# Order of weight loads, and queues of one pair's C and x, in a fused Mamba-2 scan and bilinear feed-forward kernel

## Chip, cores and metric

The kernel runs on one core of one Trainium2 chip. The metric is the device time of one execution in microseconds (us). Three runs of the kernel before gave 122.89, 122.69 and 123.45 us, median 122.89.

## What is computed

The inputs are `x` (4 batches, 8 heads, 768 tokens, 32 channels), a decay `a` per token, `B` and `C` (16 states per token and head), and three weights of a feed-forward layer. The first half is a state-space scan. The reference runs it in chunks of 32 tokens:

```python
for c in range(nc):                                   # chunks of the sequence
    cum = np.cumsum(la, axis=-1)                      # la = log a of the chunk
    L = np.exp(cum[..., :, None] - cum[..., None, :]) * causal
    M = np.einsum('bhin,bhjn->bhij', Cc, Bc) * L
    y[:, :, sl] = M @ xc + einsum('bhin,bhnd->bhid', Cc, state) * exp(cum)[..., None]
    state = decay_full * state + sum_j Bc[j] (x) xc[j] * decay_from_j[j]
```

The second half takes all heads of a token as one row of 256 numbers and gives `(row @ w_a) * (row @ w_b) @ w_out`, with 1536 hidden columns. The output is 3072 rows of 256.

## The kernel before, in words

The kernel cuts the sequence into 6 blocks of 128 tokens (instead of chunks of 32) and the 4 batches into two pairs of batches. A "pair" p = 2 * block + (batch pair) is the unit of the scan, so there are pairs 0 to 11. Pairs 0 to 3 (blocks 0 and 1) go one by one; later ones go block by block. The change touches pairs 2 and 3 and what stands around them.

For a pair of blocks 0 and 1 the stages are these.

- Loads: B, C and x each come in two transfers, one for each batch (`load1`, L157, transfers recorded at L165).
- `scale_bc` (L370, recorded at L379) multiplies B by the inverse decay (result `bm`) and C by the decay (result `cm`). For pairs 2 and 3 GpSimd does this.
- `transposes` (L386, recorded at L409) turns `bm` and `cm` on TensorE, two matmuls with the identity each, into a PSUM bank. ScalarE copies B out twice (`bt`, L413), VectorE copies C out (`ct`, L429). An argument `between` is called between the turn of B and the turn of C; whatever it issues on TensorE stands between them.
- `scores` (L437, recorded at L458) makes 32 small matmuls of turned B and C into four banks, SC[0] to SC[3]. `mask` (L490) multiplies them by the causal mask: three quarters by VectorE (L497), the last quarter by a ScalarE copy and GpSimd (L494, L495).
- `scale_x` (L357) rounds x to 16 bits. For pair 3 it is GpSimd's work (L368), for pair 2 ScalarE's (L366).
- `pv` (L555) multiplies with the carried state (L562), with x (L518), and makes the pair's own state (`ds_mm`, L545). `state_sums` (L646) and `state_spread` (L658, GpSimd, recorded at L662 and L677) carry the state on.

For the feed-forward half, `unit(p, k2)` (L726) makes two of the 12 hidden slices of a pair: four matmuls with Wa (`aps`), four with Wb (`bps`, all at L691), a ScalarE copy of the first (`asb`, L715) and a product by VectorE (`hk`, L722). `out_mm` (L734, recorded at L737) multiplies `hk` by Wo. Wo is loaded in two halves (`load_wo`, L219, recorded at L220): half 0 holds hidden slices 0 to 5, half 1 slices 6 to 11. Three of the output products of pairs 0 and 1 are made in two passes: first 18 matmuls with half 0, then, after `pv(2)`, 18 with half 1.

The order of the work is written by hand (`manual_schedule`): each engine executes its own instructions in the order of the source, and semaphores hold an instruction until its operands are there. GpSimd and SyncE also issue transfers in that order, and a transfer that waits holds what is queued behind it. For the stretch of interest that order, before the change, is:

- GpSimd: B and C of pair 2 (four transfers), three small state factors `hr`, `hs`, `hsx` (L909 to L911), Wo half 0, x of pair 2 (two transfers), the scalings of pair 2, Wo half 1, the spread of pair 0's state, x of pair 3 (two transfers, in `scores2`), the masked quarter of pair 2, four transfers that spread decay rows (`spread_rows`, L339), the scalings of pair 3, the spread of pair 1's state, and the rounding of pair 3's x.
- SyncE: the decay rows to memory (L334), then B of pair 3, which waits by an explicit dependence until Wo half 0 has landed, C of pair 3, and the C and B of later blocks (`rq` at L183, `bn` at L174).
- TensorE: the state factors' matmul into `gps` (L931), the state matmuls of pairs 0 and 1 (L545), units of pair 0, turn of B and of C of pair 2, unit (1, 3) and so on.

Of the kernel before, what the change touches and what calls it, by code (L numbers as in the profile page):

```python
# [29 lines left out]
def kernel(  # L30
# [13 lines left out]
    nc = tc.nc  # L44
# [34 lines left out]
    indm = c32[:, 0:128]  # L79
# [8 lines left out]
    Wa = [big.tile([128, 2, KC], f16, name=f"Wa{t}") for t in range(2)]  # L88
    Wb = [big.tile([128, 2, KC], f16, name=f"Wb{t}") for t in range(2)]
# [24 lines left out]
    hsx = big.tile([128, nb, NG], f32, name="hsx")  # L114
# [23 lines left out]
    def bank(name):  # L138
        return psf.tile([128, 512], f32, name=name, tag=f"ff{next(banks)}")
# [17 lines left out]
    def load1(eng, p, which, bt, i0=0, n=64):  # L157
        blk, bp = divmod(p, NBP)
        if p >= P0:
            return eng.dma_start(  # L160
                by_token(pair_in[p][which])[:, bt],
                (B, C, x)[which][2 * bp + bt, :, blk * Q : (blk + 1) * Q, :].rearrange("h q n -> q h n"),
            )
        src = (B, C, x)[which][2 * bp + bt, :, blk * Q + 2 * i0 : blk * Q + 2 * i0 + 2 * n, :]
        return eng.dma_start(  # L165
            pair_in[p][which][64 * bt + i0 : 64 * bt + i0 + n].rearrange("i h r n -> i h (r n)"),
            src.rearrange("h (i r) n -> i h (r n)", r=2),
        )
# [50 lines left out]
    def load_wo(half):  # L219
        return nc.gpsimd.dma_start(  # L220
            Wo[:, 6 * half : 6 * half + 6].rearrange("p (g kk) e -> p g (kk e)", kk=3),
            moe_w_out.rearrange("(g p kk) e -> p g (kk e)", p=128, kk=3)[:, 2 * half : 2 * half + 2],
        )
# [146 lines left out]
    def scale_bc(p, which, eng, factor=None):  # L370
        blk, bp = divmod(p, NBP)
        name = ("bm", "cm")[which]
        if p >= P0:
            f = (fBl, fCl)[which][:, blk - P0 // NBP].rearrange("p (b t h) -> p b t h", b=NBP, t=2)[:, bp]
        else:
            f = (f_c(blk) if which else fB[:, blk])[:, :, bp]
        raw = by_token(pair_in[p][which]) if p >= P0 else pair_in[p][which].rearrange("p h r n -> p r h n")
        m_ = pre.tile([128, 2, H, N], f16, name=name, tag=name, bufs=4 if which else None)
        eng.tensor_tensor(  # L379
            out=m_,  # L380
            in0=raw,
            in1=(f if factor is None else factor).unsqueeze(3).broadcast_to((128, 2, H, N)),
            op=ALU.mult,
        )
        st.setdefault(p, {})[name] = m_
    def transposes(p, ps=None, between=None, apart=False):  # L386
        s = st.setdefault(p, {})
        blk, bp = divmod(p, NBP)
        if p >= P0:
            if by_block(blk, 0):  # L390
                TB = st[("turned", p, 0)].rearrange("p t q -> p (t q)")
            else:
                tr = bank("tr").bitcast(f16)
                TB, TC = tr[:, 0:256], tr[:, 256:512]
        elif ps is None:
            ps = [bank("tb") if p == 1 else SC[0], SC[2] if p == 3 else SC[1]] if apart else None
            on_dve = apart
            TB, TC = (TT[:, 0:256], TT[:, 256:512]) if ps is None else [t_.bitcast(f16)[:, 0:256] for t_ in ps]
        else:
            on_dve = True  # L400
            TB, TC = [t_.bitcast(f16)[:, 0:256] for t_ in ps]
        BT = mid.tile([128, 2, 2, 2, 64], f16, name="bt", tag="bt")
        if not by_block(blk, 1):
            CT = mid.tile([128, 2, Q], f16, name="ct", tag="ct")
        b_ = []

        def turn(T_, src):
            for r in range(2):
                nc.tensor.transpose(T_[:, r * 128 : (r + 1) * 128], src[:, r].rearrange("p h n -> p (h n)"), ident)  # L409

        def copy_bt(e):
            o_ = BT[:, e].rearrange("p r t i -> p (r t i)")
            b_.append(nc.scalar.activation(out=o_, in_=TB, func=AF.Copy, scale=par[:, e : e + 1]))  # L413

        if not by_block(blk, 0):
            turn(TB, s["bm"])
        if between:
            between()
        if not by_block(blk, 1):
            turn(TC, s["cm"])  # L420
        copy_bt(0)
        copy_bt(1)
        if p >= P0:
            if not by_block(blk, 1):
                nc.scalar.copy(CT.rearrange("p t q -> p (t q)"), TC)
                s["CT"] = CT
            s["BT"] = BT.rearrange("p e r t i -> p e r (t i)")
            return
        c_ = (nc.vector.tensor_copy if on_dve else nc.scalar.copy)(  # L429
            CT.rearrange("p t (i r) -> p r (t i)", r=2), TC.rearrange("p (r c) -> p r c", r=2)  # L430
        )
        if apart:
            for i_ in b_:
                tc.declare_no_dep(c_.ins, i_.ins.name, reason="reads of two banks")
        s["BT"], s["CT"] = BT, CT
# [92 lines left out]
    def ds_mm(p, c0, banks):  # L528
        s = st[p]
        s["DS"] = [b_[:, c0 : c0 + 2 * D] for b_ in banks]  # L530
        for bt, m in itertools.product(range(2), range(4)) if p >= P0 else ():
            nc.tensor.matmul(
                s["DS"][bt][32 * m : 32 * m + 32, :],
                s["bm"][:, bt, 2 * m : 2 * m + 2, :].rearrange("p h n -> p (h n)"),
                by_token(s["X16"])[:, bt, 2 * m : 2 * m + 2].rearrange("p h d -> p (h d)"),
                start=True,
                stop=True,
                skip_group_check=True,
                tile_position=(0, 32 * m),
            )  # L540
        for r in range(2) if p < P0 else ():
            for m in range(4):
                for bt in range(2):
                    k = slice(64 * bt, 64 * bt + 64)
                    nc.tensor.matmul(  # L545
                        s["DS"][bt][32 * m : 32 * m + 32, :],
                        s["bm"][k, r, 2 * m : 2 * m + 2, :].rearrange("p h n -> p (h n)"),
                        s["X16"][k, 2 * m : 2 * m + 2, r, :],
                        start=(r == 0),
                        stop=(r == 1),  # L550
                        skip_group_check=True,
                        tile_position=(64 * bt, 32 * m),
                    )
# [159 lines left out]
    def evac_a(a_ps, on_dve=False):  # L713
        asb = ffh.tile([128, 512], f32, name="asb", tag="asb", bufs=5)
        (nc.vector.tensor_copy if on_dve else nc.scalar.copy)(asb, a_ps)  # L715
        return asb

    def times(p, k2, b_ps, asb):
        s = st[p]
        if "hk" not in s:  # L720
            s["hk"] = ffh.tile([128, NK, 2 * Q], f16, name="hk", tag="hk")
        nc.vector.tensor_tensor(  # L722
            out=s["hk"][:, 2 * k2 : 2 * k2 + 2, :].rearrange("p k q -> p (k q)"), in0=b_ps, in1=asb, op=ALU.mult
        )
# [97 lines left out]
    def loads_x(p, eng=None):  # L822
        if p < NP:
            load2(eng or nc.gpsimd, p, 2)
# [7 lines left out]
    def go(*items):  # L832
        for p, k2 in items:
            unit(p, k2)()
# [55 lines left out]
    asb = [evac_a(aps[0])]  # L890
# [15 lines left out]
    nc.scalar.copy(maskbd, headm.unsqueeze(2).broadcast_to((128, H, D)))  # L906
    over_mid(2, NBLK)
    times(0, 0, bps[0], asb[0])
    nc.gpsimd.tensor_tensor(out=hr, in0=Pr[:, 0:NG, Q - 1], in1=rmid[:, 0:NG], op=ALU.mult)  # L909
    nc.gpsimd.tensor_tensor(out=hs, in0=hr, in1=Pr[:, 1:NBLK, 63], op=ALU.mult)  # L910
    nc.gpsimd.tensor_tensor(  # L911
# [2 lines left out]
        in1=selb.rearrange("p (b g) -> p b g", b=nb),  # L914
        op=ALU.mult,
    )
    wo0 = load_wo(0)
    for bt in range(2):
        load1(nc.gpsimd, 2, 2, bt)
    times(0, 1, bps[1], asb[1])  # L920
    times(0, 2, bps[2], asb[2])
    scale_bc(2, 0, nc.gpsimd)
    scale_bc(2, 1, nc.gpsimd)
    load_wo(1)
    go((1, 0))
    unit(1, 1, ps=(SC[0], None))()
    late_rows(nc.vector)
    rows = store_rows(nc.sync)
    go((1, 2))
    gps = SC[0][:, 256 : 256 + nb * NG]  # L930
    nc.tensor.matmul(gps, indm, hsx.rearrange("p b g -> p (b g)"), start=True, stop=True, skip_group_check=True)  # L931
    for p in range(NBP):
        ds_mm(p, 2 * D * p, SC[:2])
    nc.scalar.copy(G.rearrange("p b g -> p (b g)"), gps)
    state_sums(0)
    state_sums(1)
    state_spread(0)
    b3 = [load1(nc.sync, 3, 0, bt) for bt in range(2)]
    tc.add_manual_dep(b3[0].ins, wo0.ins.name, AFTER, reason="weights ahead of pair 3's inputs")
    for bt in range(2):  # L940
        load1(nc.sync, 3, 1, bt)
    loads_bc(4)
    loads_bc(5)
    aps = [unit_mm(0, 3, Wa), unit_mm(0, 4, Wa)]
# [1 line left out]
    for k2 in (3, 4):  # L946
        times(0, k2, unit_mm(0, k2, Wb), asb[k2 - 3])
    go((0, 5))
    transposes(2, apart=True)
    go((1, 3))  # L950
    def scores2():
        scores(2)
        loads_x(3)
        mask(product(2, 3), by_pool=True)
        spread_rows(nc.gpsimd, rows)

# [236 lines left out]
```

## Time and profile before

| | us |
|---|---|
| median of three runs | 122.89 |
| the profiled execution, its own time | 123.49 |
| the span of its instructions | 121.8 |
| TensorE matmul busy (PE) | 116.1 |
| VectorE busy (DVE) | 93.9 |
| ScalarE busy (ACT) | 76.0 |
| GpSimd busy (POOL) | 70.3 |

The profile shows one execution. PE is TensorE's matmul row and PEld its weight loads; DVE, ACT, POOL and SP are VectorE, ScalarE, GpSimd and SyncE; a q behind an engine's name is its queue of transfers. A row of the timeline has start, duration, engine, source line, operation, the result's name and, after `<-`, the operands, how many instructions are merged in the row, and in brackets how long the engine was idle before it and what ended that. Starts count from the first instruction. A matmul's end is modelled and reaches into the next one's start, so distances between starts are the safer measure. A row of the window sums has the window's length, the busy time of each engine, the granted TensorE clock (1.00 is full) and the share of time that the core's 16 DMA engines were busy. A row of the issues has a transfer's result and source, the issuing queue, the count, the size of one, and the time from issue to landing. The granted clock is 1.00 in every window used here.

### The profile page before, as it was taken

To read this page: it belongs to the slowest core of one execution; us is meant where nothing else is said; L and a number is where in the kernel's file an instruction comes from. 1 tells how busy PE (TensorE), PEld (TensorE's weight loads), DVE (VectorE), ACT (ScalarE), POOL (GpSimd) and SP (SyncE) were. 2 spreads that over 40 slices of the span, in tenths; PEclk is the share of its full clock that TensorE was granted. 3 is DMA by queue.
4 is the path that set the end of the run, shared out by engine and by line. 5 is a ranking of instruction groups with operands and counts; after the bars stand their busy time and mean duration, and the time that the engine had idled before them with its cause. 6 is when DMAs were issued, how large, how long until landed. Compare 5 with 4: busy or idle time off the path is not lost.

```text
span 121.8 us, 3715 instructions
## 1 busy us (share of the span) xinstructions
PE 116.1 (95%) x1436; PEld 78.9 (65%) x1436; DVE 93.9 (77%) x185; ACT 76.0 (62%) x155; POOL 70.3 (58%) x96
## 2 busy tenths in 40 slices
PE   6899799999999999999999999999999999999990
PEld 2255699887898898744476464766464784555890
DVE  4999999892999979699995999996898444847200
ACT  0448866936568855987659757767757737556220
POOL 7987999894999999099999089219034000000000
DMA  3999979992579675686459901011101012010132
GB/s 64 194 153 216 210 164 220 148 180 61 81 72 206 87 84 107 131 87 130 97 188 208 312 14 43 0 48 46 43 0 43 5 43 86 0 43 0 47 88 86
DMA packets 35985, 12.29 MB, mean 101 GB/s; under 512 B 29840, under 2 KB 35248, under 8 KB 35968
## 3 DMA queue, kind: packets, MB, share of 16 engines
q1 hardware_dynamic: 30976, 6.58, 26.7%
q0 software_dynamic: 2720, 5.05, 20.7%
q10 hardware_dynamic: 2272, 0.43, 1.8%
q8 instruction: 11, 0.18, 0.6%
q14 instruction: 6, 0.05, 0.1%
HBM read 11.20 MB, written 3.21 MB: 118 GB/s over the span
## 4 chain that ended last, share of the span: by engine, by line
PE 74%; DMA 11%; POOL 4%; DVE 4%; SPq 2%; ACT 1%; issue 1%; POOLq 0%; DVEq 0%
PE ops L794 18%; PE aps L769 17%; PE bps L769 17%; PE ops L737 6%; DMA Wo<-in_moe_w_out_dram 5%; DMA cn<-in_C_dram 4%; PE aps L691 4%; PE bps L691 4%; PE SC L443 2%; DVE t L497 2%; PE SC L503 2%; DMA a_sb<-in_a_dram 2%; SPq L165 2%; POOL bn L165 1%; POOL cn L165 1%; PE SC L458 1%
## 5 line engine op out<-in xcount | busy, mean ns | idle before, releaser
L715 ACT COPY asb<-aps 128x512 f32<-128x512 f32 x71 | 41.5, 587 | 13.8 <-PE aps L769 9.3
L779 DVE TENSOR_TENSOR hkb<-bps,asb 128x512 f16<-128x512 f32 x48 | 31.9, 686 | 10.3 <-ACT asb L715 9.7
L769 PE MATMUL aps<-XB,Wa 128*128 128x512 f16 x96 | 28.6, 379 | 0.0
L769 PE MATMUL bps<-XB,Wb 128*128 128x512 f16 x96 | 28.5, 379 | 0.0
L794 PE MATMUL ops<-Wo,hkb 128*128 128x256 f16 (+1 forms) x204 | 22.6, 267 | 0.0
L794 PEld LDWEIGHTS <-hkb 128*128 128x128 f16 x204 | 18.5, 98 | 3.0
L497 DVE TENSOR_TENSOR t<-SC,causal_q 128x512 f16<-128x512 f32 x24 | 15.5, 681 | 2.4 <-PE SC L443 2.4
L769 PEld LDWEIGHTS <-Wb 128*128 128x128 f16 x96 | 9.9, 103 | 10.9
L722 DVE TENSOR_TENSOR hk<-bps,asb 128x512 f16<-128x512 f32 x24 | 15.7, 681 | 1.6 <-ACT asb L715 1.2
L495 POOL TENSOR_TENSOR t<-tmp,causal_q 128x512 f16<-128x512 f32 x8 | 9.2, 1159 | 13.1 <-ACT tmp L494 12.9
L769 PEld LDWEIGHTS <-Wa 128*128 128x128 f16 x96 | 9.7, 103 | 9.0
L806 ACT ACTIVATE osb<-ops 128x256 f32<-128x256 f32 (+1 forms) x16 | 6.0, 376 | 11.3 <-PE ops L794 11.2
L691 PE MATMUL bps<-X2T,Wb 128*128 128x256 f16 x84 | 12.4, 272 | 0.0
L368 POOL TENSOR_SCALAR x<-xn 128x512 f16<-128x512 f32 x8 | 11.9, 1489 | 0.7
L691 PE MATMUL aps<-X2T,Wa 128*128 128x256 f16 x80 | 11.9, 273 | 0.0
L737 PE MATMUL ops<-Wo,hk 128*128 128x256 f16 x96 | 11.6, 273 | 0.3 <-DMA Wo<-in_moe_w_out_dram 0.3
L737 PEld LDWEIGHTS <-hk 128*128 128x128 f16 x96 | 9.1, 98 | 1.4 <-issue 0.3
L691 PEld LDWEIGHTS <-Wb 128*128 128x128 f16 x84 | 8.6, 103 | 0.5
L691 PEld LDWEIGHTS <-Wa 128*128 128x128 f16 x84 | 8.3, 104 | 0.7
L497 DVE TENSOR_TENSOR t<-SC,causal 128x512 f16<-128x512 f32 x13 | 8.2, 677 | 0.4 <-PE SC L458 0.3
L494 ACT COPY tmp<-SC 128x512 f32<-128x512 f32 x11 | 6.5, 593 | 1.9 <-PE SC L443 0.9
L202 DVE STREAM_TRANSPOSE tq<-mq 128x256 f16<-128x256 f16 x10 | 7.4, 742 | 0.1
(108 smaller groups left out, 141.8 us busy)
## 6 DMA issues: line engine op xcount, KB each, us to landing
out_dram<-osb SPq DMA_DIRECT2D x18, 128.0 KB, 2.7
xn<-in_x_dram POOLq DMA_DIRECT2D x6, 256.0 KB, 5.1
rq<-in_C_dram SPq DMA_DIRECT2D x32, 32.0 KB, 2.7
Wo<-in_moe_w_out_dram POOLq DMA_DIRECT2D x2, 384.0 KB, 6.4
bn<-in_B_dram SPq DMA_DIRECT2D x6, 128.0 KB, 4.2
out_dram<-osb SPq DMA_DIRECT2D x11, 64.0 KB, 1.5
xn<-in_x_dram POOLq DMA_DIRECT2D x4, 128.0 KB, 5.4
xn<-in_x_dram SPq DMA_DIRECT2D x2, 256.0 KB, 5.3
```

Of the source, the lines that this page charges most:

```text
L202: nc.vector.transpose(t_.rearrange("p t (i g) -> p g t i", g=4), st[("scaled", blk, which)][:, :, 2 * bp : 2 * bp + 2].rearrange("p g t e ...
L368: eng.tensor_scalar(xo, xi, XS, None, ALU.mult)
L494: nc.scalar.copy(tmp, i_)
L495: nc.gpsimd.tensor_tensor(out=o_, in0=tmp, in1=c_, op=ALU.mult)
L497: nc.vector.tensor_tensor(out=o_, in0=i_, in1=c_, op=ALU.mult)
L691: nc.tensor.matmul(ps[:, kk * 2 * Q : (kk + 1) * 2 * Q], w_up(W, k, f), X2T[:, p, :, f], start=(f == 0), stop=(f == 1), skip_group_check=True,
L715: (nc.vector.tensor_copy if on_dve else nc.scalar.copy)(asb, a_ps)
L722: nc.vector.tensor_tensor(out=s["hk"][:, 2 * k2 : 2 * k2 + 2, :].rearrange("p k q -> p (k q)"), in0=b_ps, in1=asb, op=ALU.mult)
L737: nc.tensor.matmul(o_ps[:, 0:d_model], hk[:, k, bt * Q : (bt + 1) * Q], Wo[:, k, :], start=(k == 0), stop=(k == NK - 1), skip_group_check= ...
L769: nc.tensor.matmul(t_, w_up(W, k, f), XB[:, blk - P0 // NBP, f].rearrange("p t j q -> p (t j q)"), start=(f == 0), stop=(f == 1), skip_gro ...
L779: return lambda: nc.vector.tensor_tensor(out=s["hk"][:, k], in0=ps[1], in1=asb, op=ALU.mult)
L794: nc.tensor.matmul(o_ps[:, 0:w], hk[:, k, c * Q : (c + 1) * Q], Wo[:, k, cs], start=(k == 0), stop=(k == NK - 1), skip_group_check=True,)
```

## The change

Six edits, all before pair 3's scores; nothing is added and nothing is removed, and the same instructions run.

1. Wo half 0 is issued ahead of `hr`, `hs`, `hsx` on GpSimd.
2. Wo half 1 is issued ahead of pair 2's two scalings on GpSimd.
3. The `gps` matmul stands behind the state matmuls of pairs 0 and 1 instead of ahead of them.
4. SyncE's two transfers of pair 3's C become two transfers of pair 3's x.
5. GpSimd's two transfers of pair 3's x become two transfers of pair 3's C, at the same place in its order.
6. The turn of pair 2's C stands behind the four Wa matmuls of unit (1, 3) instead of ahead of them, and goes to bank SC[2] instead of SC[1].

```diff
-            ps = [bank("tb") if p == 1 else SC[0], SC[2] if p == 3 else SC[1]] if apart else None
+            ps = [bank("tb") if p == 1 else SC[0], SC[1] if p == 1 else SC[2]] if apart else None
...
     times(0, 0, bps[0], asb[0])
+    wo0 = load_wo(0)
     nc.gpsimd.tensor_tensor(out=hr, in0=Pr[:, 0:NG, Q - 1], in1=rmid[:, 0:NG], op=ALU.mult)
...
-    wo0 = load_wo(0)
     for bt in range(2):
         load1(nc.gpsimd, 2, 2, bt)
     times(0, 1, bps[1], asb[1])
     times(0, 2, bps[2], asb[2])
+    load_wo(1)
     scale_bc(2, 0, nc.gpsimd)
     scale_bc(2, 1, nc.gpsimd)
-    load_wo(1)
...
-    nc.tensor.matmul(gps, indm, hsx.rearrange("p b g -> p (b g)"), start=True, stop=True, skip_group_check=True)
     for p in range(NBP):
         ds_mm(p, 2 * D * p, SC[:2])
+    nc.tensor.matmul(gps, indm, hsx.rearrange("p b g -> p (b g)"), start=True, stop=True, skip_group_check=True)
...
-    for bt in range(2):
-        load1(nc.sync, 3, 1, bt)
+    loads_x(3, nc.sync)
     loads_bc(4)
...
-    transposes(2, apart=True)
-    go((1, 3))
+    a_ps = []
+    transposes(2, between=lambda: a_ps.append(unit_mm(1, 3, Wa)), apart=True)
+    asb = evac_a(a_ps[0])
+    times(1, 3, unit_mm(1, 3, Wb), asb)
     def scores2():
         scores(2)
-        loads_x(3)
+        for bt in range(2):
+            load1(nc.gpsimd, 3, 1, bt)
         mask(product(2, 3), by_pool=True)
```

## Prediction

> **What bounds the kernel now.** I read the page first, then the window sums, to see where TensorE (PE) is not busy, and then the timelines of the engines around those places.
>
> ```profile
> span 121.8 us, 3715 instructions
> PE 116.1 (95%) x1436; PEld 78.9 (65%) x1436; DVE 93.9 (77%) x185; ACT 76.0 (62%) x155; POOL 70.3 (58%) x96
> ```
>
> ```profile
> 17.00:19.00 2.00, 2.00 (x50) 1.84 (x49) 2.00 (x5) 1.28 (x4) 1.98 (x4) 1.00 0.50 73
> ...
> 24.00:27.00 3.00, 2.72 (x71) 2.42 (x69) 2.93 (x8) 0.96 (x3) 3.00 (x5) 1.00 1.11 204
> 27.00:30.00 3.00, 3.00 (x28) 2.48 (x27) 1.05 (x3) 1.90 (x5) 1.21 (x3) 1.00 0.26 54
> 30.00:31.20 1.20, 0.97 (x11) 0.85 (x10) 0.62 (x2) 0.90 (x3) 1.20 (x2) 1.00 0.30 68
> 31.20:119.00 87.80, 87.76 (x1002) 58.36 (x1000) 68.42 (x120) 57.56 (x116) 43.70 (x50) 1.00 0.38 81
> ```
>
> TensorE bounds it: from 31.20 to 119.00 us it is busy for 87.76 of 87.80 us. What comes earlier at 31.2 therefore comes earlier at the end, if the other engines keep up. The change begins at 15.7 us, where GpSimd's order first differs. Between there and 31.2 TensorE idles in two places, 0.28 us in 24 to 27 and 0.23 us in 30 to 31.2. TensorE's timeline names both.
>
> ```profile
> 17.36 0.30 PE L931 MATMUL SC<-hsx,c 128*128 128x20 f32 x2
> ...
> 20.46 0.28 PE L409 MATMUL SC<-ident,bm 128*128 128x128 f16 x2
> ...
> 26.32 0.32 PE L545 MATMUL SC<-x,bm 64*32 64x64 f16 x16
> 26.92 2.13 PE L737 MATMUL ops<-Wo,hk 128*128 128x256 f16 x18 [0.28 <-DMA Wo<-in_moe_w_out_dram]
> 28.88 0.60 PE L691 MATMUL aps<-X2T,Wa 128*128 128x256 f16 x4
> 29.32 0.27 PE L409 MATMUL SC<-ident,bm 128*128 128x128 f16 x2
> 29.43 0.60 PE L691 MATMUL bps<-X2T,Wb 128*128 128x256 f16 x4
> 30.25 0.28 PE L409 MATMUL SC<-ident,cm 128*128 128x128 f16 x2 [0.23 <-POOL cm L379]
> ...
> 36.23 0.32 PE L545 MATMUL SC<-x,bm 64*32 64x64 f16 x16
> 36.48 0.62 PE L691 MATMUL aps<-X2T,Wa 128*128 128x256 f16 x4
> 37.48 0.28 PE L409 MATMUL tr<-ident,bm 128*128 128x128 f16 x2
> ```
>
> The first wait is for Wo half 1, the second for pair 3's scaled C. Ends of matmuls are modelled, so I size both by starts. From the 16 state matmuls to the next matmul it is 36.48 - 36.23 = 0.25 us where nothing is awaited, and 26.92 - 26.32 = 0.60 here: the Wo wait costs **0.35 us**. Four Wa or Wb matmuls take 29.32 - 28.88 = 0.44, and 30.25 - 29.43 = 0.82 stands there: the wait for C costs **0.38 us**. Together 0.73 us is all that the change can win on TensorE.
>
> **The change part by part.** GpSimd, SyncE's queue, and the landings:
>
> ```profile
> 14.31 1.39 POOL L165 DMA_DIRECT2D cn<-in_C_dram  x2
> 15.68 0.24 POOL L909 TENSOR_TENSOR hr<-Pr,rmid 32x5 f32<-32x5 f32 x1
> ...
> 16.26 0.21 POOL L911 TENSOR_TENSOR hsx<-hs,c 32x20 f32<-32x20 f32 x1
> 16.50 0.74 POOL L220 DMA_DIRECT2D Wo<-in_moe_w_out_dram  x1
> ...
> 18.64 0.64 POOL L379 TENSOR_TENSOR bm<-bn,fB 128x256 f16<-128x256 f32 x1
> 19.23 0.62 POOL L379 TENSOR_TENSOR cm<-cn,fC 128x256 f16<-128x256 f32 x1
> 19.79 0.74 POOL L220 DMA_DIRECT2D Wo<-in_moe_w_out_dram  x1
> ...
> 22.02 1.43 POOL L165 DMA_DIRECT2D xn<-in_x_dram  x2
> ...
> 24.86 2.32 POOL L339 DMA_DIRECT2D Pq<-rows  x4
> 28.58 0.61 POOL L379 TENSOR_TENSOR bm<-bn,fB 128x256 f16<-128x256 f32 x1 [1.40 <-DMA bn<-in_B_dram]
> 29.58 0.62 POOL L379 TENSOR_TENSOR cm<-cn,fC 128x256 f16<-128x256 f32 x1 [0.39 <-DMA cn<-in_C_dram]
> ...
> 31.77 1.51 POOL L368 TENSOR_SCALAR x<-xn 128x512 f16<-128x512 f32 x1
> ...
> 36.79 0.63 POOL L379 TENSOR_TENSOR bm<-bn,fBl 128x256 f16<-128x256 f32 x1
> ```
>
> ```profile
> 22.25 1.29 SPq L165 DMA_DIRECT2D bn<-in_B_dram  x2
> 23.60 1.33 SPq L165 DMA_DIRECT2D cn<-in_C_dram  x2
> ```
>
> ```profile
> Wo<-in_moe_w_out_dram POOLq DMA_DIRECT2D x1, 384.0 KB, 5.7
> ...
> Wo<-in_moe_w_out_dram POOLq DMA_DIRECT2D x1, 384.0 KB, 7.1
> ...
> xn<-in_x_dram POOLq DMA_DIRECT2D x2, 128.0 KB, 5.5
> ...
> bn<-in_B_dram SPq DMA_DIRECT2D x1, 64.0 KB, 5.5
> ...
> cn<-in_C_dram SPq DMA_DIRECT2D x2, 64.0 KB, 5.1
> ...
> xn<-in_x_dram SPq DMA_DIRECT2D x1, 128.0 KB, 6.3
> ```
>
> *Wo half 0 ahead of the factors (edit 1).* It is issued at 15.69 instead of 16.50, 0.81 us earlier, and lands at about 15.69 + 5.7 = 21.4 instead of 22.2. That pays only if the transfers have room: in 17 to 19 us the DMA engines are busy 0.50 of the time, so there is some. Bounds: 0 to 0.81 us earlier; I take 0.8. `hr` to `hsx` move back by one issue, 0.74, and `hsx` ends at 16.47 + 0.74 = 17.21. The `gps` matmul wanted it at 17.36 and stands behind 32 small matmuls now (edit 3), so it waits for nothing. Cost 0.
>
> *Wo half 1 ahead of pair 2's scalings (edit 2).* Issued at 18.64 instead of 19.79, 1.15 us earlier. With the longer landing of 7.1 us it is there at 25.75. TensorE asks for it at 26.32 + 0.25 = 26.57, so the 0.35 us go, with 0.8 us to spare. What is queued behind it on GpSimd: `bm` and `cm` of pair 2 shift by 0.74, `bm` to 19.38-20.02 and `cm` to 19.97-20.59. TensorE turns B at 20.46: 0.44 us of cover is left, and without it every further delay of `bm` would be a delay of TensorE. C was turned 0.11 us behind B and would be late now; edit 6 puts four matmuls, 0.44 us, between, so C is asked for at 20.46 + 0.11 + 0.44 = 21.01, 0.42 us after `cm`. Everything on GpSimd from the state's spread on stands where it was, since the sum of what precedes it is the same. Cost 0; bounds 0 to 0.1 us of loss, if an issue on GpSimd takes that much longer than its cover.
>
> *Pair 3's B (SyncE, behind Wo half 0).* It is issued when Wo has landed: 21.4 instead of 22.25; its second transfer was issued at 22.9 and took 5.5, so it lands at about 27.6 instead of 28.4. GpSimd issues the four row transfers until 24.86 + 2.32 = 27.18, so `bm` of pair 3 runs from 27.7 to 28.3 instead of 28.58 to 29.19. With the Wo wait gone TensorE turns this B at 29.32 - 0.35 = 28.97: 0.6 us of cover. This step is needed: with `bm` at 29.19 the gained 0.35 would be lost again here.
>
> *Pair 3's C by GpSimd (edit 5).* Issued from 22.02, where x was, so its second transfer starts about 22.75 and lands, with the 5.5 us that x took there, at 28.25. From SyncE its second transfer started about 24.3 and took 5.1, landing at 29.4. No row has this C from this queue at this place. It is half of x's bytes, so I keep x's time. `cm` then follows `bm` without a wait, 28.3 to 28.9. TensorE asks for C at 28.97 + 0.11 + 0.44 = 29.52: the 0.38 us go, with 0.6 us to spare.
>
> On this the rule in the Trainium skill, "SBUF — State Buffer", section "SBUF: two separate sides", speaks against the edit: a transfer issued by GpSimd has its descriptors written by GpSimd, and VectorE can shut GpSimd out of the port for that. By it C could come late from this queue where SyncE's would not. The trace shows no sign: the two issues of x take 1.43 us here and the two of C 1.39 us at 14.31.
>
> *Pair 3's x by SyncE (edit 4).* Its two issues stand where C's stood, 1.35 us behind B's: 22.8 and 23.45. Bounds for landing: C's 5.1 us and the 6.3 us that an early x took from this queue, so 28.6 to 29.8. GpSimd rounds x 2.19 us after it starts `cm` (31.77 - 29.58), that is at 28.3 + 2.19 = 30.5. Cost 0, with at least 0.7 us to spare. The loads of later blocks are queued behind x as they were behind C.
>
> *After 31 us.* GpSimd is the tight engine: pair 4's `bm` ends at 36.79 + 0.63 = 37.42, and TensorE turns it at 37.48. If TensorE is 0.73 us earlier, GpSimd must be too. It starts `cm` of pair 3 at 28.3 instead of 29.58, 1.28 us earlier, so this holds.
>
> **The sum.** 0.35 + 0.38 = 0.73 us. The profiled execution took 123.49 us for a span of 121.8, so its own time becomes 122.76. It is 0.60 us above the median of the runs, 122.89; the median becomes 122.16, I say **122.2 us**, 0.6% faster.
>
> **The rivals.**
>
> *B does not come earlier.* The DMA engines are busy (1.11 in 24 to 27), and Wo half 1, C and B all want them. If B lands at 28.4 as before, `bm` runs 28.58 to 29.19, TensorE turns B at 29.25 instead of 28.97, and C when `cm`, right behind `bm`, has ended at 29.8: at 29.85 (as `cm`'s end at 29.58 + 0.62 = 30.20 stands 0.05 ahead of 30.25). Gain 30.25 - 29.85 = 0.40: 122.5 us. For it: the 5.5 us are mostly contention. Against it: 0.50 in 17 to 19, and Wo half 1 out of the way sooner. The Trainium skill, "DMA: Bandwidth & Descriptors", section "Issuing engines are not separate DMA queues", is on this rival's side: all queues run on the same 16 engines, so swapping queues moves no byte faster.
>
> *Nothing is won.* The change doesn't do what it says: Wo half 0 lands at 22.2 as before and C comes from GpSimd at 29.4. Then C is turned at 30.25 as before: 122.9 us. Equally, x landing as late as 31.8 would hold GpSimd's queue until pair 4's `bm` is as late as it is now; above 31.77 - 0.73 = 31.04 it begins to cost. Against it: C is issued 1.5 us earlier than before (22.75 against 24.3).
>
> *Slower.* C comes late from GpSimd, held off by VectorE.
>
> ```profile
> 23.48 1.88 DVE L497 TENSOR_TENSOR t<-SC,causal 128x512 f16<-128x512 f32 x3
> ```
>
> If the second transfer starts only when this run of products ends, at 25.36, it lands at 25.36 + 5.5 = 30.86, 1.46 us later than C did before, and TensorE turns C that much later than at 30.25: 122.9 + 1.4 = 124.3 us. It decides from a landing of 29.4 on, above which the turn is later than before. Against it stand the 1.43 us of x's issues.
>
> **How the numbers follow.** Full gain 0.64, B not earlier 0.17, nothing won 0.12, slower 0.07. A measurement of this kernel tells about 1% from no change, 1.2 us; all but the last case lie within it. Faster by over 1% would need 0.5 us more than the two waits hold: 0.04. Slower by over 1% is the upper half of the last case: 0.04. Within: 0.92. The range has the runs' scatter below the full gain (122.89 to 122.69 is 0.2, with as much again for a wait that I have not seen) and above it the cases down to nothing won: 121.7 to 123.0.
>
> **What would show it.** In the changed profile TensorE has no wait for Wo ahead of the second 18 matmuls and none for pair 3's `cm`; B of pair 3 is issued by SyncE near 21.4, C lands by 28.9, x by 30.5; `bm` and `cm` of pair 3 run back to back by 28.9; TensorE's scores of pair 3 start 0.7 us earlier. Wrong would be a new wait at the turn of pair 2's B, at the turn of pair 3's C, or of GpSimd for x.

## The result, and the profile after

| | before | after |
|---|---|---|
| median, us (21 runs each) | 123.22 | 122.66 |
| range of the runs, us | 122.69 to 124.86 | 122.42 to 123.27 |
| the profiled execution, us | 123.49 | 122.42 |
| span of that execution, us | 121.8 | 120.7 |

The ratio is 0.9955, with a 95% interval of 0.9941 to 0.9969: 0.55 us less, with 0.38 to 0.73 us inside the interval. The changed kernel was timed twice more, beside the experiments: 0.9973 (0.9958 to 0.9988) and 0.9954 (0.9938 to 0.9969).

The window sums of the changed kernel:

```profile
17.00:19.00 2.00, 2.00 (x49) 1.70 (x48) 2.00 (x7) 1.31 (x4) 1.90 (x4) 1.00 0.98 135
...
24.00:27.00 3.00, 3.00 (x74) 2.63 (x72) 2.93 (x8) 0.99 (x3) 2.98 (x6) 1.00 0.92 191
...
30.00:31.20 1.20, 1.20 (x42) 0.85 (x40) 1.20 (x3) 1.07 (x3) 1.20 (x1) 1.00 0.36 71
```

TensorE is busy all the time in the two stretches where it idled 0.28 and 0.23 us. The share of the DMA engines in 17 to 19 us rose from 0.50 to 0.98. Leaving experiment 9 aside, it is 0.95 to 1.00 in all six profiles with the first half of Wo issued early and 0.39 to 0.75 in the seven without, so the earlier Wo fills what was empty. TensorE's timeline, at the places shown of before:

```profile
16.60 0.60 PE L691 MATMUL bps<-X2T,Wb 128*128 128x256 f16 x4
17.13 0.31 PE L545 MATMUL SC<-x,bm 64*32 64x64 f16 x32
17.37 0.40 PE L933 MATMUL SC<-hsx,c 128*128 128x20 f32 x2
17.61 1.03 PE L691 MATMUL aps<-X2T,Wa 128*128 128x256 f16 x8
...
20.23 0.28 PE L409 MATMUL SC<-ident,bm 128*128 128x128 f16 x2
...
26.08 0.32 PE L545 MATMUL SC<-x,bm 64*32 64x64 f16 x16
26.34 2.14 PE L737 MATMUL ops<-Wo,hk 128*128 128x256 f16 x18
...
28.75 0.28 PE L409 MATMUL SC<-ident,bm 128*128 128x128 f16 x2
...
29.30 0.28 PE L409 MATMUL SC<-ident,cm 128*128 128x128 f16 x2
...
30.38 0.43 PE L458 MATMUL SC<-ct,bt 32*64 32x128 f16 x32
...
36.42 0.27 PE L409 MATMUL tr<-ident,bm 128*128 128x128 f16 x2
```

and the scores of pair 3 in the kernel before:

```profile
31.34 0.43 PE L458 MATMUL SC<-ct,bt 32*64 32x128 f16 x32
```

From the 16 state matmuls to the matmuls with Wo it is 26.34 - 26.08 = 0.26 us (0.60 before), and from B's turn to C's 29.30 - 28.75 = 0.55 (0.93 before): both waits are gone. GpSimd, SyncE and three landings:

```profile
15.61 0.76 POOL L220 DMA_DIRECT2D Wo<-in_moe_w_out_dram  x1
...
18.67 0.72 POOL L220 DMA_DIRECT2D Wo<-in_moe_w_out_dram  x1
...
22.04 1.41 POOL L165 DMA_DIRECT2D cn<-in_C_dram  x2
...
24.65 2.32 POOL L339 DMA_DIRECT2D Pq<-rows  x4
26.99 0.63 POOL L379 TENSOR_TENSOR bm<-bn,fB 128x256 f16<-128x256 f32 x1
27.57 0.62 POOL L379 TENSOR_TENSOR cm<-cn,fC 128x256 f16<-128x256 f32 x1
...
29.75 1.51 POOL L368 TENSOR_SCALAR x<-xn 128x512 f16<-128x512 f32 x1
```

```profile
21.89 1.73 SPq L165 DMA_DIRECT2D bn<-in_B_dram  x2
23.67 1.30 SPq L165 DMA_DIRECT2D xn<-in_x_dram  x2
```

```profile
Wo<-in_moe_w_out_dram POOLq DMA_DIRECT2D x1, 384.0 KB, 7.0
...
bn<-in_B_dram SPq DMA_DIRECT2D x1, 64.0 KB, 4.2
...
cn<-in_C_dram POOLq DMA_DIRECT2D x1, 64.0 KB, 3.7
```

`bm` and `cm` of pair 3 run back to back from 26.99 on, with no wait in front of them: what they wait for is now GpSimd's own queue (the row transfers end at 26.97), and no longer a landing.

**How much of the 1.07 us between the two profiles is the change.** The stretch from the turn of pair 2's B to pair 3's scores holds both waits. It is 30.38 - 20.23 = 10.15 us here and 31.34 - 20.46 = 10.88 before, a difference of 0.73 us. Pair 4's B is then turned 36.42 - 30.38 = 6.04 us later, before 37.48 - 31.34 = 6.14: 0.10 more, a wait for GpSimd that I had not counted. Ahead of the stretch the changed kernel loses 0.10 us at the `gps` matmul (experiment 8). The rest, about 0.3 us, comes from ahead of what the change touches: the first Wb matmuls begin at 12.59 us here and at 12.87 before, when a weight transfer lands that both kernels issue alike, and the last ones ahead of `gps` at 16.60 and 16.92.

In every profile but that of experiment 9 (92.4), an execution takes 92.0 to 92.2 us more than the start of pair 3's scores (123.49 - 31.34 = 92.15 before, 122.42 - 30.38 = 92.04 after). So that one start decides the time.

### The profile page after: what moved, and what is told of

Read it like the earlier page. It is cut to its first block, busy times and chain, and to the rows that moved or that the text cites. A ratio compares the mean times of both kernels' runs of the same rounds, so it can differ in the third digit from the quotient of the medians.

```text
span 120.7 us, 3716 instructions
## 1 busy us (share of the span) xinstructions
PE 115.5 (96%) x1436; PEld 78.8 (65%) x1436; DVE 93.9 (78%) x185; ACT 75.9 (63%) x155; POOL 70.3 (58%) x96
## 4 chain that ended last, share of the span: by engine, by line
PE 87%; DMA 5%; POOL 4%; issue 0%; ACT 0%; DVE 0%
PE ops L794 18%; PE aps L769 17%; PE bps L769 17%; PE ops L737 9%; PE bps L691 8%; PE aps L691 8%; DMA Wb<-in_moe_w_b_dram 5%; PE SC L443 2%; PE SC L503 2%; PE bps L704 1%; POOL bn L165 1%; POOL cn L165 1%; PE SC L518 1%; PE SC L593 1%; POOL Wa L213 1%; PE tr L409 1%
## 5 line engine op out<-in xcount | busy, mean ns | idle before, releaser
L794 PEld LDWEIGHTS <-hkb 128*128 128x128 f16 x204 | 18.5, 98 | 3.0
```

The lines of the kernel that those rows point to most:

```text
L794: nc.tensor.matmul(o_ps[:, 0:w], hk[:, k, c * Q : (c + 1) * Q], Wo[:, k, cs], start=(k == 0), stop=(k == NK - 1), skip_group_check=True,)
```

## The experiments

The edits are numbered as in the section on the change. Behind each ratio (to the kernel before, run beside it) stands its 95% interval. It reaches 0.15 to 0.3% to either side (0.5% in experiment 9), so that most of these ratios cannot be told from their neighbours, and the profiles carry the argument. "The stretch" is the one from pair 2's turn of B to pair 3's scores.

**1. The kernel before again, two more profiles** (no edit).

> A second look at the kernel before, nothing changed. Theory (the two waits are a property of its order): idle time ahead of the second 18 products with Wo and ahead of the turn of pair 3's C stands again, together 0.5 to 0.8 us, so its scores of pair 3 start 18.3 to 18.5 us behind the first Wb matmul, where the changed kernel needs 17.8. Rival (the first profile caught a slow one, since it took 123.49 us where the median of all runs is 123.1): one of the two waits or both are absent or under 0.2 us, and the distance is 18.0 us or less.

> A third look at the kernel before, as the second: 0.5 to 0.8 us of waits by the theory, under 0.3 us by the rival.

These executions took 124.61 and 123.13 us. TensorE in the first of them, and then in the second:

```profile
20.54 0.28 PE L409 MATMUL SC<-ident,bm 128*128 128x128 f16 x2
...
26.39 0.32 PE L545 MATMUL SC<-x,bm 64*32 64x64 f16 x16
27.23 2.12 PE L737 MATMUL ops<-Wo,hk 128*128 128x256 f16 x18 [0.51 <-DMA Wo<-in_moe_w_out_dram]
...
31.38 0.28 PE L409 MATMUL SC<-ident,cm 128*128 128x128 f16 x2 [0.89 <-POOL cm L379]
...
32.47 0.43 PE L458 MATMUL SC<-ct,bt 32*64 32x128 f16 x32
```

```profile
26.39 2.14 PE L737 MATMUL ops<-Wo,hk 128*128 128x256 f16 x18
...
28.91 0.60 PE L691 MATMUL bps<-X2T,Wb 128*128 128x256 f16 x4
29.89 0.29 PE L409 MATMUL SC<-ident,cm 128*128 128x128 f16 x2 [0.38 <-POOL cm L379]
...
30.98 0.43 PE L458 MATMUL SC<-ct,bt 32*64 32x128 f16 x32
```

The landing of pair 3's second C transfer in each (issued at 25.03 and at 24.66 us):

```profile
cn<-in_C_dram SPq DMA_DIRECT2D x1, 64.0 KB, 5.5
```

```profile
cn<-in_C_dram SPq DMA_DIRECT2D x1, 64.0 KB, 4.4
```

The stretch takes 32.47 - 20.54 = 11.93 us and, from 20.28 in the second, 10.70, that is 1.78 and 0.55 us over the 10.15 of the changed kernel. Theory and rival are each half right. The distance from the first Wb matmul was 20.04 and 18.41 us, so the first lies above the theory's 18.3 to 18.5. The wait for C stands in all three profiles of the kernel before, but its size is that of the landing: C is turned 0.8 us after it lands, at 30.25, 31.38 and 29.89 for landings at 29.4, 30.6 and 29.1. In each of the three the chain to this landing begins with Wo half 0: SyncE waits until it has landed, issues B and C one after the other (2.0 us), and C takes 4.4 to 5.5 us. The wait for Wo stands in two of the three: Wo half 1, issued at 19.8 to 20.2, landed at 26.9, 27.2 and 25.3, and TensorE asks for it at about 26.4 to 26.6. In the first of the two new profiles B was late as well: `bm` ended at 29.71 and the turn of B came at 29.77, 2.54 us behind the matmuls with Wo, where it is 2.40 and 2.41 in the two others.

**2. The changed kernel twice more** (no edit).

> The changed kernel itself, on the same chip as the three others, for comparison. Theory: the two waits are gone again and the ratio is 0.9955 as measured. Rival (the profile of the changed kernel was 1.1 us shorter in its span because of an early landing of Wb that day): waits gone again, but a span of 121 us or more where Wb lands late, with the same ratio of the times.

> The changed kernel beside these. Theory: no wait behind the first Wb matmul, 17.8 us from there to the scores of pair 3, ratio 0.995 to 0.998. Rival (the profiles so far were lucky): a wait for Wo or for pair 3's C shows here too.

Ratios 0.9973 (0.9958 to 0.9988) and 0.9954 (0.9938 to 0.9969); the profiled executions took 122.47 and 122.44 us. The stretch takes 10.15 us in both, to the hundredth as in the first profile, with no wait. The rivals did not occur: the spans were 120.8 and 120.7. The first ratio is a little worse than the theory's 0.9955, which lies just outside its interval. So in these profiles the change does not shorten a wait by a fixed amount; it takes away waits that varied between 0.55 and 1.78 us. Two things limit this. The profiled executions of the changed kernel are fast ones, the fastest of 21, the fastest of 12 and the third of 8; whether its slower executions (up to 123.27 us) wait in the stretch was not seen. And experiments 1 and 2 ran on different chips, though on the chip of experiment 1 a kernel with five of the six edits (experiment 7) also takes 10.15 us.

**3. Early Wo alone** (edits 1, 2, 3 and 6).

```diff
-    loads_x(3, nc.sync)
+    for bt in range(2):
+        load1(nc.sync, 3, 1, bt)
...
-        for bt in range(2):
-            load1(nc.gpsimd, 3, 1, bt)
+        loads_x(3)
```

> The change with C of pair 3 left on SyncE and x on GpSimd (edits 1, 2, 3 and 6 only). Theory (each wait has its own cause, and early Wo moves SyncE's whole queue): the wait for Wo half 1, 0.35 us, is gone; SyncE's B is issued at 21.9 as in the changed kernel and its C in the place of x, 23.7 and 24.3, so C lands by about 28.3, pair 3's cm ends by 28.9, and TensorE turns C at 29.3 without a wait: gain 0.6 us, ratio 0.995, nearly all of the change. Rival (the swap of queues is what brings C): C lands at 28.9 or later, a wait of 0.2 to 0.4 us stays at the turn of C, gain about 0.3 us, ratio 0.9975.

Ratio 0.9977 (0.9954 to 1.0000). The profile has the stretch at 10.15 us: C, from SyncE, landed at 27.7, and nothing waits. The mechanism came out as the theory had it, in a favourable execution: Wo half 0 landed early, so that B was issued at 20.91 and not at 21.9. The time lies where the rival put it; the theory's 0.995 is just outside the interval.

**4. The exchange of queues alone** (edits 4 and 5).

```diff
-    for bt in range(2):
-        load1(nc.sync, 3, 1, bt)
+    loads_x(3, nc.sync)
...
-        loads_x(3)
+        for bt in range(2):
+            load1(nc.gpsimd, 3, 1, bt)
```

> The kernel before with only the queues of pair 3's C and x exchanged (edits 4 and 5). Theory: the wait for Wo half 1 of 0.35 us stays; B still lands near 28.4 and C, from GpSimd, before it; cm follows bm and ends at 29.8, the turn of C stands 0.4 us earlier than before: ratio 0.997. Rival (C and B only share what the transfers have left, so C comes no earlier): no gain, ratio 1.000, and the wait for cm as before.

Ratio 0.9985 (0.9964 to 1.0005), which holds both theory and rival. In the profile C landed at 26.4, 2.7 us or more ahead of the three of before, and the stretch is again 10.15 us. My theory missed that Wo would not be waited for: Wo half 1 landed at 25.4 in this execution,

```profile
Wo<-in_moe_w_out_dram POOLq DMA_DIRECT2D x1, 384.0 KB, 5.3
```

issued at 20.06 as in the kernel before, where it took 5.5 to 7.1. So with the order of before TensorE would not have waited for Wo in this execution either. The exchange removes the wait for C, which no longer stands behind Wo half 0 and B; about Wo this run says nothing.

**5. Wo half 1 alone** (edits 2 and 6).

```diff
-    scale_bc(2, 0, nc.gpsimd)
-    scale_bc(2, 1, nc.gpsimd)
     load_wo(1)
+    scale_bc(2, 0, nc.gpsimd)
+    scale_bc(2, 1, nc.gpsimd)
```

Edit 6 is shown in the section on the change.

> The kernel before with Wo half 1 ahead of pair 2's scalings and pair 2's C turned behind four matmuls (edits 2 and 6 only). Theory (the landing of pair 3's B and C binds next): no wait for Wo, but B still waits for Wo half 0 and is issued at 22.2, C behind it; if they land at 28.4 and 29.4 as in the first profile, TensorE waits at the turns of B and C and ends as before, ratio 1.000. Rival (half 1 out of the way lets B and C land a microsecond sooner, as all transfers share the engines): B by 27.3, C by 28.5, no wait, ratio 0.996.

Ratio 0.9996 (0.9970 to 1.0021), as the theory had it. The profile, of the fastest of its 12 executions, stands between theory and rival: no wait for Wo, B and C sooner than in the first profile of before, and C still late.

```profile
28.84 0.60 PE L691 MATMUL bps<-X2T,Wb 128*128 128x256 f16 x4
29.50 0.28 PE L409 MATMUL SC<-ident,cm 128*128 128x128 f16 x2
```

```profile
cn<-in_C_dram SPq DMA_DIRECT2D x1, 64.0 KB, 4.0
```

C, issued at 24.73, landed at 28.7 and was turned 0.81 us later, 0.22 us behind the 0.44 that the four matmuls take. The stretch is 10.47 us; the other 0.1 us over 10.15 lies in the first 18 matmuls with Wo. Removing the Wo wait alone leaves C to bind next.

**6. All but the early first half** (edits 2, 4, 5 and 6), twice.

```diff
+    nc.tensor.matmul(gps, indm, hsx.rearrange("p b g -> p (b g)"), start=True, stop=True, skip_group_check=True)
     for p in range(NBP):
         ds_mm(p, 2 * D * p, SC[:2])
-    nc.tensor.matmul(gps, indm, hsx.rearrange("p b g -> p (b g)"), start=True, stop=True, skip_group_check=True)
```

Beside that, `wo0 = load_wo(0)` goes back behind `hr`, `hs` and `hsx`.

> The changed kernel with Wo half 0 behind the state factors again and the gps matmul ahead of the state matmuls again (edits 2, 4, 5 and 6 only). Theory: B is issued 0.8 us later than in the changed kernel, lands at about 27.6 instead of 26.8, and bm of pair 3 still ends at 28.3, ahead of its turn at 28.7, so nothing waits; and the stretch of gps and state matmuls takes 0.90 us again where the changed kernel's profile has 1.01, so it is 0.0 to 0.1 us faster than the changed kernel: ratio to the kernel before 0.994 to 0.995. Rival (the early first half is needed): B lands at 28.2 or later, TensorE waits 0.2 to 0.4 us at the turn of B: ratio 0.997.

> Edits 2, 4, 5 and 6 a second time, because the first time (ratio 1.000) and its profile (no wait at all behind the first Wb matmul) pointed different ways. Theory (its profile is typical and the time was drawn high by late landings of Wb): no wait behind the first Wb matmul again, 17.7 us from there to the scores of pair 3, and a ratio of 0.996 to 0.998 like the changed kernel's. Rival (the early first half of Wo is needed in most executions): a wait at the turn of pair 3's B or C in this profile, or a ratio of 0.9995 or more again.

Ratios 1.0003 (0.9981 to 1.0024) and 0.9977 (0.9958 to 0.9996); the profiled executions took 123.14 and 122.33 us. Both profiles have the stretch at 10.15 to 10.16 us, without a wait. The first ratio is worse than both the theory of its run (0.994 to 0.995) and its rival (0.997); the second ratio lies where the second theory put it. What differs is the start of the stretch, 20.89 and 20.11 us, and with it the time. In the first, TensorE had waited longest for a weight transfer that no edit touches:

```profile
13.31 0.62 PE L704 MATMUL bps<-X2T,Wb 128*128 128x256 f16 x4 [0.69 <-DMA Wb<-in_moe_w_b_dram]
```

In the second, the same matmuls began at 12.24. So the difference of 0.8 us between these two executions comes from ahead of the stretch, where that Wb lands; for the other runs this was not measured. Whether the early first half helps in executions where B lands late was not seen in either profile (`bm` of pair 3 ran right behind the row transfers in both), and the two ratios don't decide it.

**7. All but the later turn of pair 2's C** (edits 1 to 5).

```diff
-    a_ps = []
-    transposes(2, between=lambda: a_ps.append(unit_mm(1, 3, Wa)), apart=True)
-    asb = evac_a(a_ps[0])
-    times(1, 3, unit_mm(1, 3, Wb), asb)
+    transposes(2, apart=True)
+    go((1, 3))
```

> The changed kernel with pair 2's C turned directly behind its B again (all edits but 6). Theory (the later turn is the cover for the scalings that Wo half 1 pushed back): cm of pair 2 ends at 20.6 and C is asked for at 20.3, so TensorE waits 0.25 to 0.35 us there; what was won later is partly lost, ratio 0.998 to 0.999. Rival (a wait here is made up by the later waits, since C of pair 3 binds in absolute time): the wait shows, but the scores of pair 3 start no later than in the changed kernel, ratio 0.997.

Ratio 0.9995 (0.9966 to 1.0024). The profile shows no wait, against my theory:

```profile
20.62 0.28 PE L409 MATMUL SC<-ident,bm 128*128 128x128 f16 x2
20.73 0.27 PE L409 MATMUL SC<-ident,cm 128*128 128x128 f16 x2
```

```profile
19.96 0.64 POOL L379 TENSOR_TENSOR cm<-cn,fC 128x256 f16<-128x256 f32 x1
```

`cm` ended at 20.60 as expected, but TensorE came 0.4 us later than in the changed kernel's profiles (20.62 against 20.19 to 20.26), again behind a late Wb. At 20.3 it would have waited about 0.3 us. That was not seen; the ratio agrees with it and does not show it.

**8. All but the move of the `gps` matmul** (every edit but 3).

```diff
+    nc.tensor.matmul(gps, indm, hsx.rearrange("p b g -> p (b g)"), start=True, stop=True, skip_group_check=True)
     for p in range(NBP):
         ds_mm(p, 2 * D * p, SC[:2])
-    nc.tensor.matmul(gps, indm, hsx.rearrange("p b g -> p (b g)"), start=True, stop=True, skip_group_check=True)
```

> The changed kernel with the gps matmul ahead of the state matmuls as before (all edits but 3). Theory (the order behind them costs 0.10 us on TensorE, 1.01 against 0.90 us in every profile so far, and hsx now ends at 17.2): where Wb lands late, the stretch takes 0.90 us again; where it lands early, TensorE asks at 17.0 and waits up to 0.2 us for hsx; ratio within 0.001 of the changed kernel's. Rival (the 0.10 us is not the order's): 1.01 us again.

Ratio 0.9979 (0.9965 to 0.9994), where the changed kernel beside it has 0.9954 (0.9938 to 0.9969); medians 122.67 and 122.45 us. The theory had the two within 0.001.

```profile
16.55 0.60 PE L691 MATMUL bps<-X2T,Wb 128*128 128x256 f16 x4
17.23 0.40 PE L931 MATMUL SC<-hsx,c 128*128 128x20 f32 x2
17.55 0.31 PE L545 MATMUL SC<-x,bm 64*32 64x64 f16 x32
17.80 1.06 PE L691 MATMUL aps<-X2T,Wa 128*128 128x256 f16 x8
```

From the last Wb matmuls to the next Wa matmuls it is 17.80 - 16.55 = 1.25 us, against 17.61 - 16.60 = 1.01 in the changed kernel. The 0.24 us agree with the 0.22 between the medians. `hsx` ended only at 17.17 there, as Wo was issued first, and `gps` wanted it at 16.99 and began at 17.23. Edit 3 thus pays for edit 1. It has its own price: in the kernel before the same distance is 0.90 us,

```profile
16.92 0.60 PE L691 MATMUL bps<-X2T,Wb 128*128 128x256 f16 x4
...
17.82 1.05 PE L691 MATMUL aps<-X2T,Wa 128*128 128x256 f16 x8
```

It is 0.90 or 0.91 in each profile with `gps` ahead and in time, and 1.01 or 1.02 in each with `gps` behind.

**9. An attempt on the wait that is left** (the changed kernel, with pair 1's C loaded by SyncE).

```diff
+    for bt in range(2):
+        load1(nc.sync, 1, 1, bt)
     x1 = load1(nc.sync, 1, 2, 0)
...
-    for w in range(2):
-        for bt in range(2):
-            load1(nc.gpsimd, 1, w, bt)
+    for bt in range(2):
+        load1(nc.gpsimd, 1, 0, bt)
```

> The changed kernel with pair 1's C loaded by SyncE, ahead of pair 1's x, instead of by GpSimd, so that GpSimd issues the first halves of Wa and Wb 1.4 us earlier. The one wait that is left on TensorE is for this Wb (0.46 us in the changed kernel's profile). Theory (Wb's landing follows its issue): Wb lands 0.4 to 1.4 us earlier, the wait is gone, ratio to the changed kernel 0.996, to the kernel before 0.992. Rival (the transfers are full there, DMA share 1.0 to 1.2 from 3 to 15 us, so another transfer gets late in Wb's place): pair 1's x or C lands later and TensorE waits as long for them: ratio to the changed kernel 1.000 or more.

Ratio 1.0378 (1.0327 to 1.0430), median 128.30 us: the rival was right about the sign, and the loss is far larger than the wait it had in mind. Wb landed 1.3 us earlier, as the theory had it. C of pair 1 did not:

```profile
cn<-in_C_dram SPq DMA_DIRECT2D x1, 64.0 KB, 7.5
```

It was issued at 5.09 and landed at 12.6; GpSimd's landed at 8.0 in the changed kernel. GpSimd then sat at pair 1's `cm`, with the second halves of Wa and Wb queued behind it (issued from 13.33 on), and TensorE at the turn:

```profile
12.77 0.61 POOL L380 TENSOR_TENSOR cm<-cn,fC 128x256 f16<-128x256 f32 x1 [4.63 <-DMA cn<-in_C_dram]
```

```profile
13.44 0.40 PE L410 MATMUL SC<-ident,cm 128*128 128x128 f16 x2 [3.88 <-POOL cm L380]
```

No version that was measured beats the changed kernel.

## Why the prediction was right, step by step

It forecast 122.2 us, 0.6% less than before, by two waits on TensorE of 0.35 and 0.38 us. Both were there and both went; the stretch that holds them is shorter by their sum, 0.73 us. Measured were 0.33 to 0.57 us in three comparisons. The range held and the waits were the right ones; sizes of single steps were not, and some errors cancelled. By the number alone the measured 122.66 us is nearer to the rival "B does not come earlier" (122.5) than to the forecast; it is the traces that decide between them.

- *Wo half 1 issued 1.15 us earlier, in time with 0.8 us to spare.* Right: issued at 18.67, landed at 25.7 (25.75 predicted), asked for at 26.34. That the wait is 0.35 us was the reading of one execution: it is 0.6 us in the second profile of before and nothing in the third. Pair 2's scalings, behind it on GpSimd, had less cover than forecast, 0.19 and 0.16 us instead of 0.44 and 0.42, since TensorE came sooner; nothing waited.
- *Wo half 0 issued and landed 0.8 us earlier, and B with it.* Half wrong. It was issued 0.89 us earlier but took 6.3 us instead of 5.7, so B was issued at 21.89 and not at 21.4: 0.36 us earlier than before, not 0.85. In the five other profiles with the early issue B was issued between 20.36 and 22.34, in the seven without it between 22.14 and 23.01.
- *B and C of pair 3 early enough.* Right, with more room than forecast, and by luck for B. I carried over the 5.5 us of before; in the first profile B took 4.2 and C 3.7, so that B landed at 26.7 (27.6 forecast) mainly because its transfer was shorter. In the two other profiles of the changed kernel C took 3.9 and 4.9 us. What shortens these transfers was not isolated. GpSimd ran `bm` and `cm` 0.7 us sooner than predicted (28.19 for the end of `cm`, against 28.9).
- *Pair 3's x from SyncE costs nothing.* Right: GpSimd rounds it from 29.75 on (30.5 forecast) without a wait.
- *C binds if only Wo is cured.* Right, by experiment 5: the wait for Wo was gone, the wait for C stayed.
- *The `gps` matmul costs nothing behind the state matmuls.* Wrong by 0.10 us. It waits for nothing, as forecast, but the order itself costs; without edit 3 it was 0.24 us more (experiment 8).
- *After 31 us GpSimd keeps up.* Right, and here I had left out a gain: in the kernel before, pair 4's turn of B waited 0.10 us for GpSimd, and that is gone too. This and the error at `gps` cancel, by luck.
- *The forecast for the median.* Here the step that failed is the last: I took the waits of one execution for those of the median, and three runs for the median of before. The 122.66 us lie 0.46 above the forecast. Of this 0.33 us is the start, since the 21 runs of before have 123.22 and my three had 122.89; the rest is the gain, 0.56 us between the medians and not 0.69. The profiled execution took 123.49 us. With 92.15 us from the scores of pair 3 to the end, a run at the median of before has them at 31.07, 0.27 us sooner than the profiled one, by an earlier Wb or by smaller waits. The profiled execution of the changed kernel took 122.42, 0.24 us less than its median. So the two profiles stand 0.5 us further apart than the medians. That the gain in the median is about 0.2 us short of 0.73 has its likeliest reason in this; which share Wb and the waits have was not measured.

The rivals: "B does not come earlier" and "nothing is won" did not occur in any profile with the changed queues. "Slower", C held off by VectorE, did not occur: the two issues of C take 1.41 us and C lands after 3.7 us, while VectorE makes products from 21.89 to 25.13 us. The port rule of the Trainium skill, "SBUF — State Buffer", section "SBUF: two separate sides", speaks of VectorE in a 2-port mode, such as an fp32 copy within SBUF; the prediction left this condition out. No row says whether these products use such a mode, so the run shows no hold and does not test the rule.

The Trainium skill, "DMA: Bandwidth & Descriptors", section "Issuing engines are not separate DMA queues", has issuing on several engines at once save only the time to issue. The runs don't decide this, since place and time of issue moved with the queue: by the exchange alone C of pair 3 landed 2.7 us or more earlier (experiment 4), of which 1.3 to 2.0 us is its earlier issue and the rest a shorter transfer, 3.4 us where SyncE's took 4.4 to 5.5; and C of pair 1 landed 4.6 us later (experiment 9) from SyncE, issued 0.6 us later.

## What to carry to other kernels

A wait for a transfer varied from execution to execution here: read it in more than one profile before putting a number on it, and compare stretches between two fixed instructions, so that what lies ahead of the change drops out. Where two waits follow each other on the bounding engine, removing the first alone pays little if the second binds at a fixed time (experiment 5: 10.47 us for the stretch and no gain clear of noise); move what feeds both. When an issue is moved ahead of a small computation on the same queue, move the consumer of that computation back by as much (experiment 8).

## What was not expected of the hardware

- The same transfer, issued at the same place, takes 5.3 to 7.1 us (Wo half 1 at 19.8 to 20.2 us, in three profiles of before and that of experiment 4). Issued about 1.15 us sooner it landed at 25.7, 25.7 and 25.3 in the three profiles of the changed kernel.
- Four Wb matmuls, 32 small state matmuls and one float32 matmul of 20 columns take 0.90 us of TensorE's time together when the float32 one stands ahead of the small ones, and 1.01 us when it stands behind them. Why was not measured.
- After 3.88 us without work in experiment 9, TensorE's granted clock was 0.50 and then 0.55. The window sums (the clock is the last but two):

```profile
13.50:17.00 3.50, 3.50 (x61) 2.01 (x62) 2.60 (x6) 1.29 (x4) 2.54 (x4) 0.50 0.67 69
17.00:20.00 3.00, 3.00 (x46) 1.86 (x45) 1.74 (x6) 2.70 (x6) 3.00 (x6) 0.55 1.12 205
```

  The clock was 1.00 again from 20 us on. Ten Wa matmuls took 2.31 us there, and 1.27 in the changed kernel. So a late transfer of 64 KB cost its wait and a slow stretch after it, 5.3 us against the kernel before. The Trainium skill, "TensorE: Matmul & The Clock Gate", section "Part 1: The HAM clock gate (the "warmup" mystery)", has the clock fall to a half after an idle window of about 3.4 us; this run agrees.
